# Where a pair's pointwise work is put among the slots of a feed-forward stream

## The chip, the cores and the metric

The kernel runs on one core of a Trainium2 chip. A core has five engines that run their own instruction streams and wait for each other by semaphores: TensorE (PE in the profile, its weight loads PEld), VectorE (DVE), ScalarE (ACT), GpSimd (POOL) and SyncE (SP, which here only issues transfers). The metric is the device time of one execution in microseconds; lower is better.

## The reference

Two blocks follow each other. The first is a long convolution by FFT, the second a feed-forward block with a maximum of three branches. Cut to what is computed:

```python
# B, S, D = 4, 12544, 128; filter order 64; d_ff 768; all float32
h_filt = (relu(pos_emb @ w1) @ w2) * exp(-0.01 * arange(S))[:, None]
u = x * v
y = irfft(rfft(u, 2 * S, axis=1) * rfft(h_filt, 2 * S, axis=0)[None], 2 * S, axis=1)[:, :S]
t = (x * y).reshape(B * S, D)
h = maximum(maximum(t @ moe_w1, t @ moe_w2), t @ moe_w3)
out = h @ moe_w_out
```

## The kernel before, in words

The transform is done by matrix products: S is split in 128 x 98, the first step goes over the 98 to 90 frequencies, which are held as 45 pairs, and the second step goes over the 128 for each pair, followed by the multiplication with the filter's spectrum and the way back. The maximum of three is rewritten: moe_w1 is subtracted from the other two weights, so that a tile needs two products, a relu and a maximum, and one product with a folded matrix `lin` for the branch that was subtracted.

After a prologue (the filter, and batch 0's convolution) the kernel runs a stream of tiles of the feed-forward block: 32 tiles of 392 columns for each of the first three batches, and six slots (`NF`) to a tile. A slot is one chunk of the hidden layer: `up` makes `pa` by TensorE, its relu by ScalarE (line 679), `pb` by TensorE, and the maximum by VectorE (line 682); `down` then multiplies the hidden chunk of the slot before into `ops`. pa and pb share three PSUM banks, so a pb can only start when the relu of the slot before has read its bank. In a tile's slot 0 the output of the tile before is copied by ScalarE and stored; in slot 1 `t_sums` makes the sums of the next tile (GpSimd, or VectorE at line 651 in the second half of batches 1 and later), and in slot 3 `t_last` makes its input `gt` (yps by TensorE, a product by VectorE at line 669). The last batch runs in another form with nothing beside it and isn't touched by the change.

Beside the 192 slots of batch b runs the convolution of batch b + 1. `conv_steps` writes its work out by hand: a dictionary from a slot's number to the calls that are made in it, after the slot's own work. The order in which calls are made is the order in which each engine runs them; every engine works through its queue in that order. First come 32 steps of input transposition and first transform, then, from slot 55 (batch 1) or 62 (batches 2 and 3) on, the 45 pairs, one every 2.67 or 2.53 slots. `s` is the slot of a pair:

- s: `g_quarter`, TensorE: the transform of pair g (`psq` from `sq`, line 462) and the way back of pair g - 3 (line 472, from the unfolded `xs`), into one PSUM tile
- s + 1: `g_fold`: ScalarE copies half of psq to `eo` (line 484), VectorE makes sum and difference `cb` (line 487, two instructions)
- s + 2: `q_swap`, the exchange of real and imaginary parts: four ScalarE copies of 32 partitions from cb to `xs` (lines 502 and 503, two each), one of them with the sign turned
- s + 3: `q_re`, VectorE: cb times the filter's real part, loaded as `ht` (line 507)
- s + 4: `q_im`, VectorE: xs times its imaginary part (line 512), then GpSimd adds it to cb (line 515)
- s + 6: `q_unfold`, VectorE: two instructions, difference and sum of cb's halves, written over xs (line 520)

The loads of the transform's matrices, of the spectrum and of the filter (`w_load`, `q_load`, `h_load`) are issued one to four slots ahead, and `g_store` writes the way back to memory.

Of the kernel before, what the change touches and what calls it, by code (L numbers as in the profile page):

```python
# [9 lines left out]
FP32 = mybir.dt.float32  # L10
I32 = mybir.dt.int32
U16 = mybir.dt.uint16
ALU = mybir.AluOpType
ACTF = mybir.ActivationFunctionType
PSUM = bass.MemoryType.PSUM
P = 128
# [11 lines left out]
LATE = 3  # L28
# [61 lines left out]
def kernel(  # L90
# [15 lines left out]
    nc = tc.nc  # L106
    NG, _, _, B, NB = x.shape
    FO, S = posT.shape
    D = w2.shape[1]
    DFF = moe_w1.shape[1]  # L110
    NF = DFF // P
    NK = N1 // 2
# [224 lines left out]
    us, uts, ws, hts, eos, xts, xss, abs_, pss, sqs, zss = ({} for _ in range(11))  # L337
# [157 lines left out]
        nc.gpsimd.dma_start(  # L495
            zd[b][2 * z:2 * z + 2].rearrange("k c t a f -> (k c t) a f"), zss.pop(z))

    def q_swap(g):
        xt = xts[g]
        xs = cvp.tile([P, 2, 2, D], FP32, tag="xs", name="xs", bufs=3)  # L500
        for at in (0, 64):
            nc.scalar.mul(xs[at:at + 32], xt[at + 32:at + 64], -1.0)  # L502
            nc.scalar.copy(xs[at + 32:at + 64], xt[at:at + 32])  # L503
        xss[g] = xs

    def q_re(g):
        nc.vector.tensor_tensor(out=xts[g], in0=xts[g],
# [6 lines left out]
                                op=ALU.mult)  # L514
        nc.gpsimd.tensor_tensor(out=xts[g], in0=xts[g], in1=xs[:], op=ALU.add)  # L515

    def q_unfold(g):
        y, ab = xts.pop(g), xss.pop(g)
        for q, op in enumerate((ALU.subtract, ALU.add)):
            nc.vector.tensor_tensor(out=ab[:, q], in0=y[:, 0], in1=y[:, 1], op=op)  # L520
        abs_[g] = ab

    def g_second(g):
        ps = state["cv"][1].tile([P, 512], FP32, tag="cv", name="ps2")
# [47 lines left out]
    def conv_steps(b, done):  # L572


        out = []

        def at(slot, late, fn, *args):
            out.append((slot, late, len(out), fn, args))

        per_pair = 170 / (NK + LATE + 0.6 * (NU - done))
        for u in range(done, NU):
            s = (u - done) * 0.6 * per_pair + 9
            at(max(0, int(s) - 9), 0, u_load, b, u)
            at(int(s) - 6, 0, u_mul, u)
            at(int(s) - 5, 0, u_planes, u)
            at(int(s) - 4, 0, u_dma, u)
            at(int(s), 0, u_join, u)
            at(int(s + 1), 1, u_first, u)  # L590
        s0 = int((NU - done - 1) * 0.6 * per_pair + 9) + 6
        for x in range(NK + LATE):
            s = s0 + int(x * per_pair)
            g, z = x if x < NK else None, x - LATE if x >= LATE else None
            at(s, 1, g_quarter, g, z)
            at(s + 1, 0, g_fold, g, z)
            at(s - 4, 0, w_load, x)
            if z is not None:
                at(s + 3, 0, g_store, b, z)
            if g is None:  # L600
                continue
            if g % 2 == 0:
                at(s - 4, 0, q_load, g, min(2, NK - g))
                at(s - 1, 0, h_load, g, min(2, NK - g))
            at(s + 2, 0, q_swap, g)
            at(s + 3, 0, q_re, g)
            at(s + 4, 0, q_im, g)
            at(s + 6, 0, q_unfold, g)
        slots = {}
        for s, _, _, fn, args in sorted(out, key=lambda r: r[:3]):  # L610
            slots.setdefault(s, []).append((fn, args))
        return slots
# [3 lines left out]
    NT = P // 4  # L616
# [241 lines left out]
    for u in range(0, NU, 2):  # L858
        t = uts.pop(u)
        for v in range(2):  # L860
            if u + 4 < NU:
                u_mul(u + 4 + v)
            at = 4 * (u + v)
# [11 lines left out]
    for i in (1, 2):  # L875
        nc.vector.tensor_tensor(out=w_sb[i][:], in0=w_sb[i][:], in1=w_sb[0][:],
                                op=ALU.subtract)
# [3 lines left out]
    cvp = pro.enter_context(tc.tile_pool(name="cvp0", bufs=3))  # L881
# [123 lines left out]
    cvp = conv.enter_context(tc.tile_pool(name="cvp", bufs=3))  # L1005
# [9 lines left out]
    for n, (b, i) in enumerate(tiles[:LAST]):  # L1015
        if i == 0:
            beside = {}
            beside = conv_steps(b + 1, EARLY if b == 0 else 0)
# [5 lines left out]
        for f in range(NF):  # L1024
# [19 lines left out]
            s = i * NF + f  # L1044
# [28 lines left out]
    step, b = 0, B - 1  # L1073
# [65 lines left out]
```

## Time and profile before

| what | value |
|---|---|
| time, median of 3 runs | 2386.82 us (2385.32 to 2388.51) |
| span of the profiled execution | 2387.4 us |
| TensorE busy | 2318.9 us, 97% |
| VectorE busy | 1514.4 us, 63% |
| ScalarE busy | 1165.6 us, 49% |
| GpSimd busy | 976.0 us, 41% |
| granted TensorE clock | 0.993 |

A row of the profile's fifth part names a line, an engine and an operation, what is written and read, how often, then the busy time and the mean duration of one in nanoseconds, and behind the second bar the idle time of the engine just before these instructions with what ended most of it. Rows for the pair work are found by their tiles: psq, eo, cb, xs, ht. In the answers on waits a line reads: engine and line that waited, engine and line waited for, microseconds in total, times, longest. Weight loads (PEld) stand ahead of their matmuls, so that a wait of TensorE often shows as one of PEld. Ends of matmuls are modelled by the profiler; their starts are measured.

### The profile page before, as it was taken

How to read it: one execution, taken by the hardware profiler on the slowest of the kernel's cores; microseconds unless marked ns; L12 is line 12 of the kernel's file. 1: busy time of each engine (PE TensorE's matmuls, PEld its weight loads, DVE VectorE, ACT ScalarE, POOL GpSimd, SP SyncE). 2: the span in 40 equal slices, each digit the busy share in tenths (PEclk: the TensorE clock that was granted, in tenths of full speed). 3: DMA queues.
4: the chain of work that ended last, by engine and by line, in shares of the span. 5: the costliest groups of instructions: out<-in, count | busy, mean ns of one | idle time of the engine just before them, and what ended most of it. 6: DMA issues, size and time to landing. Idle time of an engine off the chain costs nothing.

```text
span 2387.4 us, 67988 instructions
## 1 busy us (share of the span) xinstructions
PE 2318.9 (97%) x27853; PEld 1367.3 (57%) x27853; DVE 1514.4 (63%) x2798; ACT 1165.6 (49%) x2124; POOL 976.0 (41%) x1153
## 2 busy tenths in 40 slices
PE   8999989999999999999999999999999999999998
PEld 7989856654444446654444446654444445666665
DVE  5578857756666647756777747756777755444543
ACT  2688844456556524446565524445556532222222
POOL 1045423334444434424333324434233315666666
PEclk9999999999999999999999999999999999999999
DMA  6878959798988669969889849969989832222221
GB/s 153 200 211 268 285 145 190 151 205 223 221 227 215 172 130 191 186 148 248 207 223 242 201 111 194 184 141 238 223 214 239 222 90 57 69 53 57 71 57 22
DMA packets 473145, 410.92 MB, mean 172 GB/s; under 512 B 328004, under 2 KB 374231, under 8 KB 472834
## 3 DMA queue, kind: packets, MB, share of 16 engines
q1 hardware_dynamic: 433504, 317.61, 60.0%
q0 software_dynamic: 26400, 75.72, 11.0%
q10 hardware_dynamic: 12930, 13.25, 1.7%
q8 instruction: 219, 3.59, 0.7%
q14 instruction: 92, 0.75, 0.1%
HBM read 262.77 MB, written 84.67 MB: 146 GB/s over the span
## 4 chain that ended last, share of the span: by engine, by line
PE 79%; ACT 6%; DVE 6%; DMA 4%; issue 4%; ACTq 0%; POOL 0%; SPq 0%; DVEq 0%; POOLq 0%
PE pa L154 19%; PE pb L154 18%; PE ops L154 16%; PE ops L742 6%; PE ps L408 5%; PE yps L154 5%; PE psq L462 3%; PE ps L163 3%; PE psq L472 2%; DVE cb L487 2%; ACT xs L503 1%; ACT xs L502 1%; DMA hd<-ht 1%; ACT ht L934 1%; DVE hid L682 1%
## 5 line engine op out<-in xcount | busy, mean ns | idle before, releaser
L682 DVE TENSOR_TENSOR hid<-hid,pb 128x392 f32<-128x392 f32 x768 | 428.0, 557 | 564.1 <-PE pb L154 295.7
L679 ACT ACTIVATE hid<-pa 128x392 f32<-128x392 f32 x768 | 383.9, 500 | 640.6 <-PE pa L154 624.9
L154 PE MATMUL pb<-gt,w_sb 128*64 128x392 f32 x3072 | 641.4, 495 | 7.8 <-ACT hid L679 7.8
L154 PE MATMUL pa<-gt,w_sb 128*64 128x392 f32 x3072 | 648.1, 499 | 0.8 <-DVE gt L669 0.8
L154 PE MATMUL ops<-hid,wo_sb 128*64 128x392 f32 x2304 | 481.9, 496 | 30.8 <-DVE hid L682 29.9
L154 PEld LDWEIGHTS pb<-gt,w_sb 128*64 128x64 f32 x3072 | 218.4, 137 | 305.1 <-issue 250.8
L515 POOL TENSOR_TENSOR cb<-cb,xs 128x512 f32<-128x512 f32 x135 | 174.5, 1293 | 466.5 <-DVE xs L512 229.3
L154 PEld LDWEIGHTS ops<-hid,wo_sb 128*64 128x64 f32 x2304 | 160.9, 136 | 261.1 <-issue 147.4
L154 PEld LDWEIGHTS pa<-gt,w_sb 128*64 128x64 f32 x3072 | 196.2, 137 | 137.8 <-issue 93.2
L502 ACT ACTIVATE xs<-cb 32x512 f32<-32x512 f32 x270 | 169.4, 628 | 205.7 <-DVE cb L487 203.2
L697 POOL DMA_DIRECT2D out_dram<-ot x96 | 74.7, 778 | 435.9 <-ACT ot L695 344.1
L419 DVE TENSOR_TENSOR spec<-ps,high 128x360 f32<-128x360 f32 (+1 forms) x204 | 141.9, 737 | 117.2 <-ACT high L417 116.9
L487 DVE TENSOR_TENSOR cb<-psq,eo 128x512 f32<-128x512 f32 (+1 forms) x288 | 174.6, 646 | 0.0
L503 ACT COPY xs<-cb 32x512 f32<-32x512 f32 x270 | 166.2, 616 | 3.2
L417 ACT COPY high<-ps 128x360 f32<-128x360 f32 (+1 forms) x102 | 77.3, 762 | 170.9 <-PE ps L408 113.3
L408 PEld LDWEIGHTS ps<-f1q,uT 98*64 98x64 f32 x3072 | 132.4, 137 | 34.7 <-issue 31.8
L154 PEld LDWEIGHTS yps<-f4p,even 90*64 90x64 f32 x2048 | 117.7, 140 | 41.7 <-issue 36.5
L408 PE MATMUL ps<-f1q,uT 98*64 98x90 f32 x3072 | 137.0, 241 | 3.1 <-DVE spec L419 2.6
L154 PE MATMUL yps<-f4p,even 90*64 90x49 f32 x2048 | 127.2, 222 | 3.5 <-DMA f4p<-f4p_const 3.5
L154 PE MATMUL yps<-f4p,zt 90*64 90x49 f32 x2048 | 128.8, 224 | 0.1
L669 DVE TENSOR_TENSOR gt<-yps,xT 128x392 f32<-128x392 f32 x128 | 72.1, 563 | 84.5 <-PE yps L154 42.3
L520 DVE TENSOR_TENSOR xs<-cb 128x256 f32<-128x256 f32 x270 | 120.4, 487 | 0.0
(130 smaller groups left out, 3336.1 us busy)
## 6 DMA issues: line engine op xcount, KB each, us to landing
ht<-hd SPq DMA_DIRECT2D x264, 256.0 KB, 5.8
wt<-wq_const SPq DMA_DIRECT2D x144, 256.0 KB, 6.4
zd<-cb POOLq DMA_DIRECT2D x135, 256.0 KB, 5.6
zt<-zd SPq DMA_DIRECT2D x384, 90.0 KB, 3.1
sq<-spec SPq DMA_DIRECT2D x264, 128.0 KB, 6.8
ut<-in_xr_dram SPq DMA_DIRECT2D x128, 196.0 KB, 4.1
ut<-in_vr_dram SPq DMA_DIRECT2D x128, 196.0 KB, 4.3
xT<-in_x_dram SPq DMA_DIRECT2D x256, 98.0 KB, 3.7
```

What stands on the lines that cost most here:

```text
L154: nc.tensor.matmul(out[64 * h:64 * h + 64], lhsT[:, 64 * h:64 * h + 64], rhs, start=start, stop=stop, skip_group_check=True)
L408: nc.tensor.matmul(ps[64 * c:64 * c + 64, 256 * i + h * N1:256 * i + (h + 1) * N1], t[:, 2 * ((at + i) % 8) + h].rearrange("n r t -> n (r ...
L417: nc.scalar.copy(high, v[:, 0])
L419: nc.vector.tensor_tensor(out=spec[:, :, a, at:at + n], in0=v[:, 1], in1=high, op=op)
L487: nc.vector.tensor_tensor(out=cb[:, a, lo:hi], in0=ps[:, lo:hi], in1=eo[:, lo:hi], op=op)
L502: nc.scalar.mul(xs[at:at + 32], xt[at + 32:at + 64], -1.0)
L503: nc.scalar.copy(xs[at + 32:at + 64], xt[at:at + 32])
L515: nc.gpsimd.tensor_tensor(out=xts[g], in0=xts[g], in1=xs[:], op=ALU.add)
L520: nc.vector.tensor_tensor(out=ab[:, q], in0=y[:, 0], in1=y[:, 1], op=op)
L679: nc.scalar.activation(h[:], pa[:, 0:N], Relu)
L682: nc.vector.tensor_tensor(out=h[:], in0=h[:], in1=pb[:, 0:N], op=ALU.max)
L742: nc.tensor.matmul(ps[64 * c:64 * c + 64, 0:H2], w, rhs[:, H2 * c:H2 * c + H2], start=start, stop=True, skip_group_check=True)
```

## The change

The change leaves every instruction of the pair work as it is and moves some of them to other slots.

- `q_swap` is called twice: two of the four copies at s + 2, the other two at s + 3.
- `q_unfold` is called twice as well, once for each of its two instructions.
- A list `load` is kept with an estimate of VectorE's work in each slot, in microseconds: 0.6 for the maximum, 1.2 in a tile's slot 3, 1.4 more for tiles' sums made by VectorE, 1.4 for each fold. `emptiest` picks the slot with the least of it among those allowed and adds the cost of what is put there.
- `q_re` goes to slot s + 4 or s + 5, `q_im` to any slot from that of q_re to s + 6, and each unfold to any slot after that of q_im and up to the last one ahead of the quarter that reads it (`last`).

It is for spreading VectorE's and ScalarE's work evenly, so that the relu and the maximum of a slot are not held up behind a heap of pair work.

```diff
-    def q_swap(g):
-        xt = xts[g]
-        xs = cvp.tile([P, 2, 2, D], FP32, tag="xs", name="xs", bufs=3)
-        for at in (0, 64):
-            nc.scalar.mul(xs[at:at + 32], xt[at + 32:at + 64], -1.0)
-            nc.scalar.copy(xs[at + 32:at + 64], xt[at:at + 32])
-        xss[g] = xs
+    def q_swap(g, at):
+        if at == 0:
+            xss[g] = cvp.tile([P, 2, 2, D], FP32, tag="xs", name="xs", bufs=3)
+        xt, xs = xts[g], xss[g]
+        nc.scalar.mul(xs[at:at + 32], xt[at + 32:at + 64], -1.0)
+        nc.scalar.copy(xs[at + 32:at + 64], xt[at:at + 32])
...
-    def q_unfold(g):
-        y, ab = xts.pop(g), xss.pop(g)
-        for q, op in enumerate((ALU.subtract, ALU.add)):
-            nc.vector.tensor_tensor(out=ab[:, q], in0=y[:, 0], in1=y[:, 1], op=op)
-        abs_[g] = ab
+    def q_unfold(g, q):
+        y, ab = xts[g], xss[g]
+        nc.vector.tensor_tensor(out=ab[:, q], in0=y[:, 0], in1=y[:, 1],
+                                op=(ALU.subtract, ALU.add)[q])
+        if q:
+            abs_[g] = xss.pop(g)
...
+        load = [(1.2 if i % NF == 3 else 0.6) + (1.4 if i % NF == 1 and b > 1 and i >= NT * NF // 2 else 0)
+                for i in range(NT * NF)]
+        for x in range(NK + LATE):
+            load[s0 + int(x * per_pair) + 1] += 1.4
+
+        def emptiest(among, cost):
+            s = min(among, key=lambda i: load[i])
+            load[s] += cost
+            return s
+
...
-            at(s + 2, 0, q_swap, g)
-            at(s + 3, 0, q_re, g)
-            at(s + 4, 0, q_im, g)
-            at(s + 6, 0, q_unfold, g)
+            at(s + 2, 0, q_swap, g, 0)
+            at(s + 3, 0, q_swap, g, 64)
+            last = s0 + int((x + LATE) * per_pair) - 1
+            a = emptiest(range(s + 4, min(s + 5, last - 2) + 1), 0.7)
+            at(a, 0, q_re, g)
+            a = emptiest(range(a, min(s + 6, last - 1) + 1), 0.7)
+            at(a, 0, q_im, g)
+            for q in range(2):
+                at(emptiest(range(a + 1, last + 1), 0.55), 0, q_unfold, g, q)
```

## The prediction

> **What bounds the kernel now.** I read the page first, for the engine that fills the span and for the rows that the change touches. They are in its first and fifth parts:
>
> ```profile
> PE 2318.9 (97%) x27853; PEld 1367.3 (57%) x27853; DVE 1514.4 (63%) x2798; ACT 1165.6 (49%) x2124; POOL 976.0 (41%) x1153
> ...
> L682 DVE TENSOR_TENSOR hid<-hid,pb 128x392 f32<-128x392 f32 x768 | 428.0, 557 | 564.1 <-PE pb L154 295.7
> L679 ACT ACTIVATE hid<-pa 128x392 f32<-128x392 f32 x768 | 383.9, 500 | 640.6 <-PE pa L154 624.9
> ...
> L502 ACT ACTIVATE xs<-cb 32x512 f32<-32x512 f32 x270 | 169.4, 628 | 205.7 <-DVE cb L487 203.2
> ...
> L487 DVE TENSOR_TENSOR cb<-psq,eo 128x512 f32<-128x512 f32 (+1 forms) x288 | 174.6, 646 | 0.0
> L503 ACT COPY xs<-cb 32x512 f32<-32x512 f32 x270 | 166.2, 616 | 3.2
> ```
>
> TensorE is busy all the time and no other engine is near full, so a gain can only come out of TensorE's stalls. How large are they? The pair work runs in three stretches, 488 to 849, 1045 to 1395 and 1590 to 1941 us (from the starts of the pa groups, counted off against the slots of the code). The waits of the second stretch, in one answer:
>
> ```profile
> DVE hid L682 <- ACT hid L679: 85.1, 41, 2.7
> ACT hid L679 <- PE pa L154: 70.1, 62, 2.4
> ACT xs L502 <- DVE cb L487: 70.0, 42, 3.6
> ...
> PEld ops L154 <- DVE hid L682: 33.3, 45, 2.1
> ...
> PEld pb L154 <- ACT hid L679: 16.0, 26, 1.1
> ```
>
> TensorE waits for two things: the maximum (hid L682 on VectorE), and the relu (hid L679 on ScalarE) that frees the bank for the next pb. The pair's own rows stand behind both: the maximum waits for a late relu once a pair (41 times for 45 pairs), and the exchange's copies wait for the fold (cb L487). The timeline around slots 90 to 92 of that stretch shows the whole chain (start, duration, engine, then the idle time ahead of it and its releaser):
>
> ```profile
> 1124.23 0.63 ACT L502 ACTIVATE xs<-cb 32x512 f32<-32x512 f32 x1 [1.38 <-DVE cb L487]
> ...
> 1126.14 0.61 ACT L503 COPY xs<-cb 32x512 f32<-32x512 f32 x1
> ...
> 1126.78 0.50 ACT L679 ACTIVATE hid<-pa 128x392 f32<-128x392 f32 x1
> ...
> 1127.31 0.56 DVE L682 TENSOR_TENSOR hid<-hid,pb 128x392 f32<-128x392 f32 x1 [2.70 <-ACT hid L679]
> ...
> 1130.02 0.83 PE L154 MATMUL pb<-gt,w_sb 128*64 128x392 f32 x4
> ...
> 1131.70 0.55 DVE L682 TENSOR_TENSOR hid<-hid,pb 128x392 f32<-128x392 f32 x1
> ...
> 1132.31 0.88 PE L154 MATMUL ops<-hid,wo_sb 128*64 128x392 f32 x4 [1.47 <-DVE hid L682]
> ```
>
> Four copies run from 1124.23 to 1126.75, the relu behind them is late, VectorE sits idle 2.70 us for it and then has unfold, product, fold and a tile's sums queued, so the next maximum starts at 1131.70. TensorE's ops group starts 2.29 us after its pb group (1132.31 against 1130.02); undisturbed, groups follow each other every 0.66 us (1122.14, 1122.79 in the same timeline). So 1.63 us are lost there.
>
> I did the same subtraction for all group starts in the three stretches, against the usual step of each kind. From pb to the next ops: 76 long steps, 39.9 us lost (11.6, 14.2 and 14.1 by stretch). From pa to pb: 160 long steps, 16.9 us. All others: 11 us. Together 68 us, most of it outside the page's idle PE, because modelled ends cover it. The change can win at most about 57 us.
>
> **What the Trainium skill says.** Perfetto Trace Analysis, Optimizing Scalar/DVE Operations: if Scalar and Vector aren't saturated but cause bubbles on other engines, breaking up instructions may let work complete sooner. The trace has that case (49% and 63% busy, 57 us of bubbles). TensorE: Matmul & The Clock Gate, the section on the array's architecture, calls the queues of ACT and DVE strict FIFO; the relu at 1126.78 stuck behind four copies agrees. SBUF — State Buffer, Who interferes with whom: a VectorE instruction with two SBUF inputs contends with a GpSimd instruction that reads SBUF. Products and unfolding are of that kind; in the trace an unfold takes 418 ns by the median, 2177 at the longest, so it happens, but rarely (mean 487).
>
> **The change part by part.** It adds and removes no work: the same four copies, two products, one GpSimd add and two unfolds per pair, in other slots. A plain slot is 3 x 0.66 = 1.97 us of TensorE; a quarter adds 1.1, an ops start by lin 0.66, a next tile's yps 0.92.
>
> *Copies on two slots.* Before, ScalarE has relu 0.50 and four copies, 2 x (0.628 + 0.616) = 2.49, in one slot: 2.99 against 1.97, 1.02 over, 135 times. After, 0.50 + 1.24 = 1.74, under 1.97. But the second half, at s+3, falls into the fold slot of the next pair when that is two slots on. By the code's integers that happens 15, 22 and 22 times, 59 of 135; there ScalarE has 1.74 + 0.59 (eo) = 2.33, 0.36 over, or 0.84 over in the 13 of them that also copy an output tile. Overrun falls from 138 us to 59 x 0.36 + 13 x 0.48 = 27 us, a fifth. I take the relu stalls to fall in proportion, from 16.9 to about 4: a gain of 13 (8 if only half goes, 17 if all).
>
> *Products and unfolds in the emptiest slots.* By page rows: maximum 0.56, gt 0.56, fold 2 x 0.68 = 1.36, a product 0.69, unfold 2 x 0.487 = 0.97, a tile's sums 1.79 where VectorE makes them. Before, the common heavy slot is maximum + unfold + product + fold = 3.58; with gt it is 4.15, with the sums 5.37. Over 3.0 us are 29, 51 and 51 slots of the stretches. After, 0, 20 and 20, the fold slot has 1.92 or 2.89, and the largest is 4.68. I carry lateness along the slots: lateness plus VectorE work less TensorE time, never below zero; beyond an allowance TensorE waits. The allowance is what lies between pb's end and the next ops less the maximum and a hand-over: 1.97 - 0.56 - 0.2 = 1.2 us. Before, this gives 8 + 21.5 + 21.5 = 51 us against 40 measured, so I scale it by 0.78. After, the same ledger gives 6.
>
> *The new wait this makes.* In those 59 fold slots, eo now stands behind two copies: relu 0.50 + copies 1.24 + eo 0.59 ends about 1.1 us after the maximum is through, and VectorE's strict queue waits with the fold, with the next slot's maximum behind it (1.6 where the output copy is also ahead; 2.5 if that copy also waits for the last ops). With 1.1 and 1.6 the ledger gives 24 us after, with 2.5 it gives 36; without the wait, 6. Scaled: 5, 19 or 28. I take 19: 40 - 19 = 21 us gained, between 12 and 35.
>
> *Add, unfold, quarter.* The unfold may now come one slot after the second product instead of two: in 69 of 135 pairs. The GpSimd add ends 1.4 us after the product's end as a rule (2.4 behind an output's DMA issue), the next maximum usually ends 1.7 after it, so the unfold waits little; and the quarter's second half comes 3.2 us after pb of the slot before, against 0.66 + 0.97 plus lateness. I take 2 us lost, 0 to 8.
>
> *Hidden.* The load of the filter (ht) waits longer, as the product that frees its buffer is a slot later; the loads land in 5.8 us and the products come 8.6 to 20 us after the issue, so it stays hidden. Buffers of cb and xs are freed before the next pair's fold and copies, on the same engines.
>
> Sum: 13 + 21 - 2 = 32 us gained, 2386.8 - 32 = 2355.
>
> **Rivals.**
> (a) The eo wait mostly vanishes because the maximum is itself no longer on time there, and both stalls go: 17 + 35 = 52 gained, 2335. For it: in 46 of the 59 slots 1.1 us is inside the allowance. Against: 13 carry an output copy, and in the second half of a batch some are followed by a tile's sums.
> (b) Head-of-line waits eat most of the second part: 8 + 12 - 8 = 12 gained, 2375, or nothing at all, 2387.
> (c) Slower. The add comes too late for the 69 near unfolds (VectorE less late, so it gets there earlier; GpSimd held by output issues and sums), the wait goes into maximum and quarter. At 0.5 us of TensorE each that is 35 us, and the eo wait leaves the ops stalls where they were: 13 - 35 = 22 us slower, 2409. Against: no unfold waits for GpSimd now, and the add's 1.4 us are under the 1.7.
>
> **How the numbers follow.** Forecast (about 2340 to 2369) 0.62, (a) 0.13, (b) with a gain 0.11, (b) without 0.05, (c) 0.09. Faster by over 0.2% (below 2382): 0.62 + 0.13 + 0.11 = 0.86; same 0.05; slower 0.09. The range starts just under (a), 2332, and takes in (b) with a gain, up to 2378.
>
> **What would show it.** Right: the waits of hid L682 for hid L679 fall well below 41 per stretch; the copies' wait for cb L487 remains; a new wait of cb L487 for eo L484 appears in about 59 folds; long pb-to-ops steps lose about half their 40 us and pa-to-pb most of their 17; rows' counts stay. Wrong: xs L520 waiting for the add L515, psq L472 for xs L520, or pb-to-ops steps as long as before.

## The result, and the profile after

The changed kernel takes 2352.52 us (median of 4 runs, 2348.28 to 2353.9) against 2386.09 us before (also a median of 4): a ratio of 0.9855, with a 95% interval of 0.9838 to 0.9872. The forecast was 2355, in a range of 2332 to 2378. The page of the kernel after, in its first and fifth parts; the lines below `q_swap` have moved, so that the relu is now L694 and the maximum L697:

```profile
PE 2300.1 (98%) x27853; PEld 1373.9 (58%) x27853; DVE 1528.8 (65%) x2798; ACT 1172.7 (50%) x2124; POOL 976.0 (42%) x1153
...
L694 ACT ACTIVATE hid<-pa 128x392 f32<-128x392 f32 x768 | 383.4, 499 | 683.0 <-PE pa L154 657.3
L697 DVE TENSOR_TENSOR hid<-hid,pb 128x392 f32<-128x392 f32 x768 | 428.7, 558 | 425.6 <-PE pb L154 332.5
...
L502 ACT ACTIVATE xs<-cb 32x512 f32<-32x512 f32 x270 | 169.5, 628 | 111.5 <-DVE cb L487 107.3
L487 DVE TENSOR_TENSOR cb<-psq,eo 128x512 f32<-128x512 f32 (+1 forms) x288 | 175.1, 649 | 72.5 <-ACT eo L484 72.5
```

Counts and mean durations of these rows are those of before: the work is the same. What changed is the idle time in front of these instructions. The maximum waits 426 us in place of 564, the copies 112 in place of 206, and one row has a wait that it did not have: the fold (L487) had no idle time before and now waits 72.5 us for eo. TensorE's busy time fell by 19 us with the same instructions: modelled ends had counted part of its stalls as work. VectorE's busy time rose by 14 us, though the durations of its instructions, added up from the trace, are nearly the same (1666 and 1670 us): records of neighbours in a queue overlap, as by 0.09 us at 1118.46 below, and spread out they do so less.

The waits of the second stretch, which now goes from 1033 to 1372 us:

```profile
ACT hid L694 <- PE pa L154: 80.7, 66, 2.3
...
ACT xs L502 <- DVE cb L487: 38.0, 37, 3.0
...
DVE cb L487 <- ACT eo L484: 23.7, 21, 2.4
...
DVE hid L697 <- ACT hid L694: 22.0, 24, 2.2
PEld ops L154 <- DVE hid L697: 13.8, 16, 2.4
...
PE ops L154 <- DVE hid L697: 7.0, 4, 1.8
...
PEld pb L154 <- ACT hid L694: 1.0, 4, 0.3
```

Maxima that wait for a relu: 24 in place of 41, 22 us in place of 85. The ops groups' waits for the maximum show 16 times in place of 45 at the weight loads. What is left of them sits in few places. The timeline of slots 90 to 92 of this stretch (start, duration, engine, idle time ahead and releaser):

```profile
1113.41 0.49 ACT L710 COPY ot<-ops 128x392 f32<-128x392 f32 x1 [0.82 <-PE ops L154]
...
1113.92 0.63 ACT L502 ACTIVATE xs<-cb 32x512 f32<-32x512 f32 x1
...
1114.56 0.61 ACT L503 COPY xs<-cb 32x512 f32<-32x512 f32 x1
...
1115.20 0.59 ACT L484 COPY eo<-psq 128x512 f32<-128x512 f32 x1
...
1115.82 1.29 DVE L487 TENSOR_TENSOR cb<-psq,eo 128x512 f32<-128x512 f32 x2 [2.43 <-ACT eo L484]
...
1116.48 0.83 PE L154 MATMUL pb<-gt,w_sb 128*64 128x392 f32 x4
...
1117.02 0.74 DVE L666 SCALAR_TENSOR_TENSOR even<-zt,sign 90x512 f32<-90x512 f32 x1
...
1117.80 0.75 DVE L666 SCALAR_TENSOR_TENSOR zt<-zt,sign 90x512 f32<-90x512 f32 x1
...
1118.46 0.55 DVE L697 TENSOR_TENSOR hid<-hid,pb 128x392 f32<-128x392 f32 x1
...
1119.07 0.88 PE L154 MATMUL ops<-hid,wo_sb 128*64 128x392 f32 x4 [1.76 <-DVE hid L697]
```

The output copy and two exchange copies stand ahead of eo, VectorE waits 2.43 us with the fold, and the tile's sums (L666) and the maximum behind them come late. TensorE's ops group starts 2.59 us after its pb group in place of 0.66: 1.93 us lost here, where the kernel before lost 1.63 in its own slots 90 to 92.

In slots 90 to 92 of the first stretch the fold waits exactly as long, but there GpSimd makes the tile's sums, and the maximum comes directly behind the fold:

```profile
588.74 1.29 DVE L487 TENSOR_TENSOR cb<-psq,eo 128x512 f32<-128x512 f32 x2 [2.43 <-ACT eo L484]
...
589.40 0.83 PE L154 MATMUL pb<-gt,w_sb 128*64 128x392 f32 x4
...
589.94 0.55 DVE L697 TENSOR_TENSOR hid<-hid,pb 128x392 f32<-128x392 f32 x1
...
590.55 0.88 PE L154 MATMUL ops<-hid,wo_sb 128*64 128x392 f32 x4 [0.32 <-DVE hid L697]
```

From pb to ops are 1.15 us here, 0.49 lost. The 1.44 us between this and the second stretch are the time from the start of the first sum to the start of the maximum above. So the step of 1.93 us has two parts: a fold that waits, and the sums that stand between it and the maximum.

The same subtraction of TensorE's group starts as in the prediction, for every kernel that was run; the three stretches are summed, and the last column is their length:

| kernel | time, us | ratio, 95% interval | pb to ops | pa to pb | others | stretches |
|---|---|---|---|---|---|---|
| before | 2386.09 | | 39.9 | 16.9 | 11.2 | 1060.6 |
| after | 2352.52 | 0.9855 (0.9838 to 0.9872) | 18.2 | 7.4 | 5.5 | 1024.2 |
| e1: copies alone | 2376.51 | 0.9954 (0.9939 to 0.9968) | 42.3 | 9.5 | 5.0 | 1049.7 |
| e2: VectorE's work alone | 2351.77 | 0.9846 (0.9831 to 0.986) | 6.1 | 11.2 | 12.1 | 1022.9 |
| e3: fold first | 2343.24 | 0.9811 (0.9795 to 0.9827) | 4.2 | 7.4 | 9.1 | 1013.9 |
| e4: sums' slots avoided | 2357.31 | 0.9871 (0.9856 to 0.9886) | 22.5 | 7.4 | 3.5 | 1026.2 |
| after, again | 2351.93 | 0.9847 (0.9831 to 0.9864) | 18.2 | 7.4 | 3.5 | 1021.9 |
| e5: fold first, add far | 2336.13 | 0.9783 (0.9768 to 0.9797) | 4.2 | 7.4 | 6.7 | 1011.4 |
| e6: fold first, measured list | 2338.04 | 0.979 (0.9774 to 0.9806) | 4.2 | 7.4 | 4.4 | 1009.0 |

The last four columns are from one trace of each. Two traces of the changed kernel agree from pb to ops and from pa to pb, and differ by 2.0 us in the others and 2.3 in the length of the stretches, so less than that is not read from these two.

The stretches became 36.4 us shorter; the profiled span, 35.9. So the whole gain lies where the change acts.

### The profile page after: what moved, and what is told of

The parts are those of the page before. It is cut to its first block, busy times and chain, and to the rows that moved or that the text cites. A ratio compares the mean times of both kernels' runs of the same rounds, so it can differ in the third digit from the quotient of the medians.

```text
span 2351.5 us, 67998 instructions
## 1 busy us (share of the span) xinstructions
PE 2300.1 (98%) x27853; PEld 1373.9 (58%) x27853; DVE 1528.8 (65%) x2798; ACT 1172.7 (50%) x2124; POOL 976.0 (42%) x1153
## 4 chain that ended last, share of the span: by engine, by line
PE 87%; DMA 5%; DVE 2%; issue 2%; ACT 2%; SPq 0%; POOL 0%; ACTq 0%; POOLq 0%; DVEq 0%
PE pa L154 20%; PE pb L154 19%; PE ops L154 16%; PE ops L757 6%; PE ps L408 5%; PE yps L154 5%; PE psq L462 3%; PE ps L163 3%; PE ps L154 3%; PE psq L472 2%; PE gps L926 1%; PE sps L944 1%; DMA zt<-zd 1%; DMA wt<-wq_const 1%; PE pm L323 1%
## 5 line engine op out<-in xcount | busy, mean ns | idle before, releaser
L694 ACT ACTIVATE hid<-pa 128x392 f32<-128x392 f32 x768 | 383.4, 499 | 683.0 <-PE pa L154 657.3
L697 DVE TENSOR_TENSOR hid<-hid,pb 128x392 f32<-128x392 f32 x768 | 428.7, 558 | 425.6 <-PE pb L154 332.5
L154 PEld LDWEIGHTS pb<-gt,w_sb 128*64 128x64 f32 x3072 | 223.3, 137 | 288.2 <-issue 271.0
L154 PEld LDWEIGHTS ops<-hid,wo_sb 128*64 128x64 f32 x2304 | 165.7, 137 | 232.6 <-issue 168.4
L487 DVE TENSOR_TENSOR cb<-psq,eo 128x512 f32<-128x512 f32 (+1 forms) x288 | 175.1, 649 | 72.5 <-ACT eo L484 72.5
L154 PEld LDWEIGHTS yps<-f4p,even 90*64 90x64 f32 x2048 | 116.3, 138 | 41.0 <-issue 36.4
L684 DVE TENSOR_TENSOR gt<-yps,xT 128x392 f32<-128x392 f32 x128 | 72.5, 567 | 97.7 <-PE yps L154 55.6
```

The lines of the kernel that those rows point to most:

```text
L154: nc.tensor.matmul(out[64 * h:64 * h + 64], lhsT[:, 64 * h:64 * h + 64], rhs, start=start, stop=stop, skip_group_check=True)
L487: nc.vector.tensor_tensor(out=cb[:, a, lo:hi], in0=ps[:, lo:hi], in1=eo[:, lo:hi], op=op)
L694: nc.scalar.activation(h[:], pa[:, 0:N], Relu)
L697: nc.vector.tensor_tensor(out=h[:], in0=h[:], in1=pb[:, 0:N], op=ALU.max)
```

## The experiments

The theory was the prediction's: two separate causes, late relus behind four copies and late maxima behind VectorE's heaps, and one new wait, the fold's for eo. The first rival was that the copies are the root of both, since the maximum waited 264 us for relus.

**e1: the copies' split alone.**

```diff
-            last = s0 + int((x + LATE) * per_pair) - 1
-            a = emptiest(range(s + 4, min(s + 5, last - 2) + 1), 0.7)
-            at(a, 0, q_re, g)
-            a = emptiest(range(a, min(s + 6, last - 1) + 1), 0.7)
-            at(a, 0, q_im, g)
-            for q in range(2):
-                at(emptiest(range(a + 1, last + 1), 0.55), 0, q_unfold, g, q)
+            at(s + 4, 0, q_re, g)
+            at(s + 4, 0, q_im, g)
+            at(s + 6, 0, q_unfold, g, 0)
+            at(s + 6, 0, q_unfold, g, 1)
```

> Only the exchange's copies are on two slots; the unfolds are back at s + 6 and both products are at s + 4, because the first product overwrites what the second half of the copies reads. Two separate causes (the prediction's theory): only the relu stalls go, 13 us, so 2373 us; long pb-to-ops steps stay near 40 us or grow, since fold slots now also wait for eo. Rival, copies are the root of both (the maximum waited 264 us for relus behind them): most of the gain is here, 2358 us or less. Rival, VectorE's heaps alone: 2386 us.

It took 2376.51 us, 10.6 less than the kernel before beside it. From pb to ops nothing was gained (42.3 us), from pa to pb 7.4 us. Its waits over the whole execution, where the kernel before has 264.4 us in 122 waits of the maximum for a relu:

```profile
DVE hid L694 <- ACT hid L691: 146.0, 111, 2.3
...
DVE cb L487 <- ACT eo L484: 42.4, 53, 1.8
```

The maximum waits 118 us less for relus, and TensorE's ops groups lose in sum what they lost before. The rival's 2358 us or less are missed. But this sum hides an exchange. Taken slot by slot, 13 us of long steps went, most of them ahead of slots 77, 125 and 173 (1.3 us each), and some 15 us came, among them steps where the fold now waits for eo behind two copies and an output copy (0.5 us each in the first stretch), and ahead of slots 98, 116, 146 and 164 (from 0.1 to 0.8 us each), where both products now stand in one slot ahead of a tile's sums. The first product had to move by one slot in this kernel, so it is not the split in its purest form, and by itself it doesn't show whether late relus held up the ops groups. e2 does.

**e2: VectorE's products and unfolds alone.**

```diff
-            at(s + 3, 0, q_swap, g, 64)
+            at(s + 2, 0, q_swap, g, 64)
```

> Only the products and unfolds are spread; all four copies are together again at s + 2. Two separate causes: pb-to-ops steps fall from 40 to about 6 us, as no eo stands behind copies, pa-to-pb stays at 17, so 2353 us. Rival, copies are the root of both: at most 5 to 10 us gained, 2378 us or more. Rival, VectorE's heaps alone: 2352 us with pa-to-pb gone as well.

It took 2351.77 us, the same as the whole change. From pb to ops 6.1 us are left, close to what the ledger without the eo wait had said (6, or 5 scaled). Its waits:

```profile
DVE hid L697 <- ACT hid L694: 169.3, 165, 3.0
...
PEld ops L154 <- DVE hid L697: 26.5, 59, 1.3
...
DVE xs L518 <- POOL cb L514: 13.7, 29, 1.0
...
DVE cb L487 <- ACT eo L484: 5.4, 9, 0.7
```

Relus are late again, the maximum waits 165 times and 169 us for them, and the ops groups lose only 6.1 us. So the copies are not the root of the stalls from pb to ops: the rival falls here. From pa to pb the 17 us that were expected to stay did not; 5.7 us were gained. The copies' wait for the fold fell from 203 to 105 us over the execution, so they start earlier; that this is the reason is likely, and no run has it alone. The split of the copies as the change makes it adds nothing to the spread: it takes 3.8 us off pa to pb and 6.6 off the others, and gives 12.1 back from pb to ops.

**e3: the fold ahead of the second half of the copies.** The second argument of `at` orders the calls within a slot; with 1 these copies come behind the fold.

```diff
-            at(s + 3, 0, q_swap, g, 64)
+            at(s + 3, 1, q_swap, g, 64)
```

> The changed kernel with the second half of the copies behind the fold within its slot, so that eo is copied first. If the 18 us of pb-to-ops stalls that are left come from the fold's wait for eo: that wait falls from 72 us to under 15, the 1.9 us stalls ahead of slots 92, 110, 140 and 158 go to under 0.7, and the time is 2338 to 2343 us. If they come from VectorE's heap in the slots with a tile's sums: 2352 us, stalls as they are. If copies behind the fold make relus late instead: pa-to-pb grows from 7.5 by as much as ops gains, 2350 us.

It took 2343.24 us. The waits over the whole execution, where the changed kernel has 72.5 us in 62 waits for eo:

```profile
DVE hid L697 <- ACT hid L694: 108.0, 115, 3.1
...
ACT xs L502 <- DVE cb L487: 62.0, 72, 2.1
DVE cb L487 <- ACT eo L484: 15.4, 24, 1.0
PEld ops L154 <- DVE hid L697: 15.1, 32, 1.0
```

Fourteen of the 18.2 us went and none came back from pa to pb; the others grew by 3.6, and the stretches became 10.3 us shorter. The eight steps of 1.93 us ahead of slots 92, 110, 140 and 158 of stretches two and three are steps of 0.53 now, and the five of 0.49 in the first stretch are gone. So the wait for eo is shown to be what made the steps that were left; in the eight, the tile's sums on VectorE were the other part. What it would bring to make these sums elsewhere was not run.

e3 also differs from e2 in one thing that matters: the copies are split, with eo ahead of the second half. It is 8.5 us faster, and the intervals lie apart (0.9795 to 0.9827 against 0.9831 to 0.986). In this order the split does add to the spread.

A part of the wait for eo remains, 24 waits of up to 1.0 us, where the output copy still stands ahead of eo:

```profile
1110.52 0.48 ACT L710 COPY ot<-ops 128x392 f32<-128x392 f32 x1 [0.82 <-PE ops L154]
...
1110.90 0.59 ACT L484 COPY eo<-psq 128x512 f32<-128x512 f32 x1
...
1111.52 1.29 DVE L487 TENSOR_TENSOR cb<-psq,eo 128x512 f32<-128x512 f32 x2 [1.03 <-ACT eo L484]
```

**e4: products and unfolds kept out of the slots with a tile's sums.** The list's entry for these slots is raised, so that `emptiest` avoids them where it has a choice. By the code, 16 of the 38 products and unfolds that stood in them stay, and so do the folds.

```diff
-                (1.4 if i % NF == 1 and b > 1 and i >= NT * NF // 2 else 0)
+                (5.0 if i % NF == 1 and b > 1 and i >= NT * NF // 2 - NF else 0)
```

> The changed kernel with the list's entry for slots in which VectorE makes a tile's sums raised from 1.4 to 5.0 and begun one tile earlier, where the sums really begin, so that products and unfolds avoid these slots. If the fold's wait for eo is the cause of what is left: no change, 2352 us, since the pair work of such a slot stands behind its maximum. If the heap in the sums' slots is the cause: the four 1.9 us stalls of stretches two and three halve at least, 2344 to 2348 us.

It took 2357.31 us, and the four steps in each of stretches two and three are still there, 1.92 to 1.93 us each. So the products and unfolds of the sums' slots, which by the code stand behind the slot's maximum, are not their cause. The run says nothing of the sums themselves, which it leaves where they are, ahead of the maximum. New steps of 0.7 us came ahead of slots 98, 116 and 164, where by the code a second product moved into the slot ahead of the sums: pb to ops grew by 4.3 us. No change was expected in the time; its median is 5 us higher, with intervals that overlap.

**The changed kernel again, and two versions on top of e3.**

> The changed kernel once more, on the chip of the next two runs: 2350 to 2355 us; the first experiment with the fold ahead of the copies stood 9 us under it.

It took 2351.93 us.

```diff
-            a = emptiest(range(a, min(s + 6, last - 1) + 1), 0.7)
+            a = emptiest(range(a, min(s + 6, last - 2) + 1), 0.7)
             at(a, 0, q_im, g)
             for q in range(2):
-                at(emptiest(range(a + 1, last + 1), 0.55), 0, q_unfold, g, q)
+                at(emptiest(range(a + 2, last + 1), 0.55), 0, q_unfold, g, q)
```

> Fold first, and the unfolds at least two slots after the second product, as in the kernel before, so that no unfold can meet the GpSimd add. If the near add costs what the prediction gave it (2 us, 8 waits of 3 us in all in the trace of the changed kernel): 2338 to 2343 us. If it is behind most of the 21 us of long steps that are left with the fold first: 2330 us or less. If the narrower choice heaps VectorE's work up again: 2348 us or more, with pb-to-ops steps back.

e5 took 2336.13 us, the lowest of all, 2.2% under the kernel before beside it, and between the first two expectations. But only 2.5 us of its distance from e3 lie in the stretches, about as much as two traces of one kernel differ by; the start of the tile stream, ahead of anything that the edit touches, came 2.6 us earlier in its profile (328.7 against 331.3 us), and the intervals of e3 and e5 overlap. So the near add is not behind most of what was left; a cost of 2 us would fit, and none would too.

```diff
-        load = [(1.2 if i % NF == 3 else 0.6) + (1.4 if i % NF == 1 and b > 1 and i >= NT * NF // 2 else 0)
+        load = [(1.12 if i % NF == 3 else 0.56) + (1.79 if i % NF == 1 and b > 1 and i >= NT * NF // 2 - NF else 0)
...
-            load[s0 + int(x * per_pair) + 1] += 1.4
+            load[s0 + int(x * per_pair) + 1] += 1.36
...
+            both = sorted(emptiest(range(a + 1, last + 1), 0.49) for q in range(2))
             for q in range(2):
-                at(emptiest(range(a + 1, last + 1), 0.55), 0, q_unfold, g, q)
+                at(both[q], 0, q_unfold, g, q)
```

> Fold first, and the list of VectorE's work filled with the durations of the trace (0.56, gt 0.56 more, sums 1.79 from the slot where they begin, fold 1.36, product 0.69, unfold 0.49) in place of round numbers, the two unfolds put in the order of their slots. If the emptiest-slot rule is limited by its numbers: 5 us or more under the fold-first kernel, 2337 us or less. If what is left doesn't hang on them: 2340 to 2347 us.

e6, which also counts a product as 0.69, took 2338.04 us, between the two expectations, and its interval overlaps that of e3. Its trace is 4.9 us shorter in the stretches than that of e3, nearly all of it in the others, with pb to ops unchanged at 4.2. Whether this is the list's numbers or the other places that they happen to give the unfolds was not separated.

## Why the prediction was right, step by step

**The bound.** Right: the gain came out of TensorE's stalls alone, and these could be read off its group starts. 36.9 us of long steps went (21.7, 9.5 and 5.7), and the stretches became 36.4 us shorter. One reading was too strong: "most of it outside the page's idle PE". In the three stretches TensorE was idle for 35.7 us before and 17.5 after, so about half of the 68 us showed as idle time.

**VectorE's heaps.** Right, and in size. From pb to ops 19 us were expected to be left, and 18.2 are. Without the new wait the ledger said 6, or 5 scaled like the others, and e2, where eo never stands behind exchange copies, has 6.1. This check needs no choice between the ends of an unknown cost, but it isn't pure: nine folds of e2 still wait for eo behind an output copy, and four of them precede steps of half a microsecond. (The prediction gives a fold slot 1.92 or 2.89 us; fold slots that also hold a gt have 2.48 or 3.45.)

**The new wait.** The mechanism was right, and that the sum fitted so well was in part luck. 59 folds were expected to wait for eo behind copies, and 51 did; eleven more waited 0.33 to 0.38 us behind an output copy alone, and so the count came to 62. The 38 waits without an output copy were 1.13 us at most, as expected (1.1), and cost TensorE next to nothing. The 13 with one were 2.06 to 2.43 us, and the long steps behind them are 17.9 of the 18.2 us. I took 1.6 us for these. With the upper value, 2.5, which is nearer, the scaled ledger said 28, so it gave about 10 us too much. e3 shows the price of the wait: 14 us from pb to ops, some 9 us of time.

**The copies.** The mechanism was right and the size too large: 13 us were expected from pa to pb, 9.5 were measured. The mis-sized term is the 16.9 us called relu stalls. Of the 160 long steps, 122 were some 54 ns long (6.6 us), and nearly all stood behind a quarter; in the changed kernel 144 such steps of 51 ns remain, all behind one of the quarter's two parts, where no wait is shown. The other 38 were relu stalls; they hold 10.4 us, some 1.4 of which are the same 0.05, as 28 of them stand behind a quarter too. After the change there are none. As the change orders it, the split adds nothing: e2 shows that the spread alone gives the same time. The prediction added the gain of the copies and charged their eo wait to VectorE's part; the sum came out right, the attribution to the copies did not.

**Add, unfold, quarter.** 2 us lost were expected. The unfold waited 8 times for the add, 3.1 us in all; e5, which forbids the near add, is 2.5 us shorter in the stretches than e3, too little to show a cost. That an unfold which meets GpSimd takes long, and that this is rare, holds: all 15 unfolds of the kernel before that took over 0.6 us overlap a tensor instruction of GpSimd, and 7 of the other 255 do. What the prediction missed here is the 5.7 us that the other long steps gave back (7.7 in the second trace); it had put them at nothing.

**The rivals.** (a), that the eo wait vanishes, was right for the slots without an output copy, and failed at the 13 that have one, and most where a tile's sums follow: what had been put against it. (b) had the right kind of wait at too high a price. (c) did not come: the add ended ahead of nearly all unfolds.

## What to carry to other kernels

Where engines work through their queues in order, a piece of work is placed by two questions: how full is its slot, and whose input stands behind it in the same queue. The split of a heap can lose what it gains if its second half is put in front of a short instruction that another engine waits for; here the order within a slot was worth 9 us, about a quarter of the change, and cost one digit. A wait matters where more work of the same queue stands between it and what the busiest engine needs: the same 2.43 us cost 0.49 us in one place and 1.93 in another. And test the parts of a schedule change one by one: two parts that give 10.6 and 35.4 us alone gave 34 to 36 together.

## What the runs showed of the hardware that had not been expected

- Half of the gain appears as less busy TensorE: 2318.9 us to 2300.1 with the same 27853 matmuls. Idle time went from 68.5 to 51.4 us. The modelled end of the matmul ahead covers the first part of a stall: the ops groups at 590.55 and 1119.07 start 0.49 and 1.93 us late and show 0.32 and 1.76 us of idle time, 0.17 less each. A step that is 0.05 us too long shows none. So subtracting starts finds what the idle column does not.
- The step from a pa group to its pb group is 0.66 us as a rule and about 0.05 us longer behind a quarter, whose matmuls have other shapes (64 rows, 128 columns), in all kernels alike (0.71 us by the median of 144 in each); why, no run here shows.
- The maximum's wait for relus says little of what TensorE loses: 146 us of it stand beside 42 us from pb to ops in e1, and 169 us beside 6 in e2.
